# Four row buffers instead of two for the partial sums, and two buffers instead of three for the late weight words

## The chip, the cores and the metric

The kernel runs on one core of a Trainium2 chip. The metric is the device time of one execution in microseconds (us). TensorE (PE) multiplies, VectorE (DVE) and ScalarE (ACT) do elementwise work and read the accumulators out, SyncE (SP) and GpSimd (POOL) only issue transfers here.

## The reference

All inputs are float32, and wide weights are handed over as float64 words and made into float32 by the kernel. For each of 8 batches and 8 heads (576 rows, head size 64, 32 memory slots):

```python
a = softmax(phi, axis=2)                 # over the 576 rows, for each memory slot
k_m = einsum('bhsm,bhsd->bhmd', a, k)    # 32 memory keys per head
v_m = einsum('bhsm,bhsd->bhmd', a, v)
attn = softmax(q @ k_m^T / 8)
x = (attn @ v_m)  rearranged to (8*576, 512)
out = (sigmoid(x @ w_gate) * (x @ w_val)) @ w_out    # 512 -> 1536 -> 512
```

The kernel never forms `x`. It multiplies `v_m` with the weights of the gate and value layers (`make_u`), so that the gate is a product of that with the attention weights.

## The kernel before

**Tiles.** The hidden width 1536 is cut into 12 tiles of 128, `f` = 0 to 11. The 576 rows of a batch `b` are cut into four full tiles of 128 rows, `t` = 0 to 3, and a tail of 64. A step is one pair `(b, f)`. Its two halves are `c` = 0 (row tiles 0 and 1) and `c` = 1 (row tiles 2 and 3 with the tail). A half does `gate_half` (12 matmuls, a sigmoid on ACT, a product on DVE, and the split of the result into a high and a low part), and `out_half` three halves later (`LAG`): six matmuls that add into the accumulators `acc[b, t]` of two row tiles in PSUM.

**Turns.** Batches 0 to 3 do not run through all 12 tiles of the hidden width at once, since the weights are still being loaded and converted. They go in turns of `TURN` = 4 steps: batches 0 to 3 with f = 0 to 3, then again with f = 4 to 7, then with f = 8 to 11. Batches 4 to 7 then run all 12 steps each. There are 96 steps in all.

**Partial sums.** At the end of a turn the four accumulators are read out into a tile `row` (128 x 512, 256 KB) and freed for the next turn. After f = 3 the row is a plain copy (L495 on ACT, L497 on DVE) and is stored to a DRAM tile `part`. After f = 7 and f = 11 the earlier `part` is loaded into a row tile, the accumulator is added to it in place (L492 on DVE), and it is stored to `part` again or, after f = 11, to the output. The helper `row_of` allots a row tile and issues that load. In before there are two row buffers. The tiles of t = 0 and 1 are allotted and loaded at the end of the next to last step of the turn:

```python
if (b, f + 1) in ends and c:
    for t in range(2):
        rows[b, t] = row_of(b, t)
```

Those of t = 2 and 3 are allotted only when `out_half` reads the accumulator out, by `rows.pop((b, t), None) or row_of(b, t)`.

**Queues.** `move` keeps two queues, each in program order: "batch" on SP (inputs, `row<-part`, and the attention weights `at_hi`, `at_lo` that are fetched back for the next turn) and "stream" on POOL (weight words, `part<-row`, `out_dram<-row`). A transfer that waits holds up those behind it on its queue.

**Weight words.** `CONVERT` says in which step each piece `(f, k)` of the weights is converted: one ACT instruction (L171) and four on DVE (L172 to L179). `load_jobs` loads the next pieces (512 KB each) when a buffer is free; a conversion's end frees one. Early pieces use four buffers. The late ones, from (8, 2) on, use `WORDS[1]` buffers. In before these are one tile of its own named `words` and two halves of the room of `q`, which nothing else uses in that stretch. The ten late pieces are (8, 2), (9, 0), (9, 1), ... (11, 2). POOL issues the first of them earlier than the program is written, because nothing makes them wait.

**Order.** PE's order is written out by hand. On DVE and ACT a scheduler places each instruction within bounds, and so a change of buffers can move instructions there.

Of the kernel before, what the change touches and what calls it, by code (L numbers as in the profile page):

```python
# [9 lines left out]
F32 = mybir.dt.float32  # L10
F32R = mybir.dt.float32r
I32 = mybir.dt.int32
# [5 lines left out]
P = 128  # L18
B, H, S, D, M = 8, 8, 576, 64, 32
DM, DFF = 512, 1536  # L20
# [3 lines left out]
SF = 4  # L24
# [11 lines left out]
QUAD = 4  # L36
TURN = 4
ALONE = 4
WORDS = (4, 3)


CONVERT = {
# [10 lines left out]
def attn_moe_kernel(  # L53
# [15 lines left out]
    mb = ctx.enter_context(tc.tile_pool(name="moe", bufs=1))  # L69
# [14 lines left out]
    def att(shape, name, bufs=1):  # L84
        return sb.tile(shape, F32, name=name, bufs=bufs)
# [11 lines left out]
    def wo_of(f):  # L97
        return [t[:, f % NE, :] for t in wos[f // NE]]
# [14 lines left out]
    def move(dst, src, queue="batch"):  # L113


        with ExitStack() as behind:
            if queue in last_move:
                behind.enter_context(tc.issue_after(last_move[queue].ins))
            last_move[queue] = queues[queue].dma_start(dst, src)  # L119
# [15 lines left out]
    def matmul(*args, **kw):  # L135
        in_turn(nc.tensor.matmul, *args, **kw)
# [6 lines left out]
    spare_room = []  # L143
# [4 lines left out]
    def load_jobs(n=None, queue="stream"):  # L148

        while jobs and (n is None or n > 0):  # L150
            f, k = jobs[0]
            room = WORDS[len(wos) - 1]
            if (k == 2 and f // NE >= len(wos)) or len(waiting) == room:
                break
            src = wo[f] if k == 2 else wgv[f][:, 2 * k : 2 * k + 2, :].rearrange("p k n -> p (k n)")
            if len(wos) == 1:
                words = pools["conv"].tile([P, 512, 2], I32, name="words", bufs=room)
            else:
                words = spare_room[0]
                spare_room.append(spare_room.pop(0))  # L160
            move(words.rearrange("p n t -> p (n t)"), src.bitcast(I32), queue)
            words_of[f, k] = words
            waiting.append(jobs.pop(0))
            n = n and n - 1

    def to_f32(dst, f, k):


        words = words_of.pop((f, k))
        low, high, bits = words[:, :, 0], words[:, :, 1], dst.bitcast(I32)  # L170
        nc.scalar.activation(dst, high.bitcast(F32), AF.Abs)  # L171
        nc.vector.tensor_scalar(dst, dst, TINY, HUGE, op0=ALU.max, op1=ALU.min)  # L172
        nc.vector.tensor_scalar(
            bits, bits, 3, 0x3FFFFFFF, op0=ALU.logical_shift_left, op1=ALU.bitwise_and
        )
        nc.vector.scalar_tensor_tensor(  # L176
            bits, high, -0x40000000, bits, op0=ALU.bitwise_and, op1=ALU.bitwise_or
        )
        last_conv[0] = nc.vector.scalar_tensor_tensor(  # L179
            bits, low, 29, bits, op0=ALU.logical_shift_right, op1=ALU.bitwise_or  # L180
        )
        waiting.remove((f, k))
        if jobs and not waiting and jobs[0][1] == 2 and jobs[0][0] // NE >= len(wos):

            early.close()
            late = ctx.enter_context(tc.tile_pool(name="late", bufs=1))
            wos[1] = [late.tile([P, NFT - NE, DM], F32R, name=f"wo2_{part}") for part in ("hi", "lo")]
            last = ctx.enter_context(tc.tile_pool(name="conv1", bufs=1))
            q_room = att([P, NKT * S], "q").bitcast(I32)
            spare_room.append(last.tile([P, 512, 2], I32, name="words"))  # L190
            spare_room.extend(
                q_room[:, i * 1024 : (i + 1) * 1024].rearrange("p (n t) -> p n t", t=2)
                for i in range(2)
            )
        load_jobs()

    def convert(f, k):
        if k == 2:
            hi, lo = wo_of(f)
            raw = mb.tile([P, DM], F32, name="wo_raw")  # L200
            to_f32(raw, f, k)
            nc.scalar.copy(hi, raw)
            rest(lo, raw, hi)
        else:
            to_f32(wg[:, f, 2 * k : 2 * k + 2, :].rearrange("p k n -> p (k n)"), f, k)
# [270 lines left out]
    def out_half(b, f, c, at_start, at_end):  # L476

        hi, lo = G.pop((b, f, c))
        w_hi, w_lo = wo_of(f)
        for j in range(2):  # L480
            t = 2 * c + j
            if at_start:
                acc[b, t] = po.tile([P, DM], F32, name=f"acc{t}")
            ts = slice(j * P, (j + 1) * P)
            o = acc[b, t]
            matmul(o, hi[:, ts], w_hi, start=at_start, stop=False)
            matmul(o, hi[:, ts], w_lo, start=False, stop=False)
            matmul(o, lo[:, ts], w_hi, start=False, stop=at_end)
            if at_end:
                st = last_rows(t) if b == B - 1 else rows.pop((b, t), None) or row_of(b, t)  # L490
                if (b, t) in part:
                    nc.vector.tensor_tensor(st, o, st, op=ALU.add)  # L492
                    part.pop((b, t))
                elif t % 2:
                    nc.scalar.copy(st, o)  # L495
                else:
                    nc.vector.tensor_copy(st, o)  # L497
                if f == NFT - 1:
                    queue = "batch" if b == B - 1 else "stream"
                    move(out[b * S + t * P : b * S + (t + 1) * P, :], st, queue)  # L500
                else:
                    part[b, t] = dram.tile([P, DM], F32, name=f"part{b}_{t}_{f}")
                    move(part[b, t], st, "stream")
                del acc[b, t]
        if (b, f + 1) in ends and c:
            for t in range(2):
                rows[b, t] = row_of(b, t)

    rows = {}
# [2 lines left out]
    def last_rows(t):  # L512

        if not room_of_last:
            room_of_last.append(att([P, SF, 512], "kvm0"))
        return room_of_last[0][:, t, :]

    def row_of(b, t):

        st = mb.tile([P, DM], F32, name="row", bufs=2)  # L520
        if (b, t) in part:
            move(st, part[b, t])
        return st
# [215 lines left out]
    for i, (b, f, at_start, at_end) in enumerate(steps):  # L739
# [20 lines left out]
        while len(pend) >= LAG:  # L760
            out_half(*pend.pop(0))
# [4 lines left out]
        while len(pend) >= LAG:  # L766
            out_half(*pend.pop(0))
# [6 lines left out]
    for half in pend:  # L774
        out_half(*half)
# [54 lines left out]
```

## Time and profile before

| what | us |
|---|---|
| runs | 788.04, 784.37, 788.99; median 788.04 |
| the profiled execution's own time | 787.27 |
| its span, from the first to the last instruction | 785.5 |
| PE busy | 737.1 (94%) |
| DVE busy | 437.5 (56%) |
| ACT busy | 334.1 (43%) |

PE is near full occupation from about 80 us on. The first 80 us are start-up. The rows below are read as "start, duration, engine, line, operation, output<-inputs, count", with the idle time ahead of the instruction and what ended it in square brackets.

### The profile page before, as it was taken

How to read it: one execution, taken by the hardware profiler on the slowest of the kernel's cores; microseconds unless marked ns; L12 is line 12 of the kernel's file. 1: busy time of each engine (PE TensorE's matmuls, PEld its weight loads, DVE VectorE, ACT ScalarE, POOL GpSimd, SP SyncE). 2: the span in 40 equal slices, each digit the busy share in tenths (PEclk: the TensorE clock that was granted, in tenths of full speed). 3: DMA queues.
4: the chain of work that ended last, by engine and by line, in shares of the span. 5: the costliest groups of instructions: out<-in, count | busy, mean ns of one | idle time of the engine just before them, and what ended most of it. 6: DMA issues, size and time to landing. Idle time of an engine off the chain costs nothing.

```text
span 785.5 us, 13710 instructions
## 1 busy us (share of the span) xinstructions
PE 737.1 (94%) x5584; PEld 608.2 (77%) x5584; DVE 437.5 (56%) x840; ACT 334.1 (43%) x789; POOL 54.3 (7%) x104
## 2 busy tenths in 40 slices
PE   6464989999999899999999999999999999999997
PEld 4343878887788688887888888878888888888886
DVE  4778576976587575455754743365234643433422
ACT  3445463746444243332633533346333433333322
POOL 0010011111111110010110000010000000010000
PEclk9786999999999999999999999999999999999999
DMA  9664826465755353344254142002000100010002
GB/s 350 277 237 156 313 112 258 129 233 179 259 173 195 129 194 128 118 151 142 68 171 166 64 133 93 1 28 88 2 1 1 54 15 1 1 55 1 1 1 68
DMA packets 27200, 93.17 MB, mean 119 GB/s; under 512 B 3520, under 2 KB 4544, under 8 KB 25088
## 3 DMA queue, kind: packets, MB, share of 16 engines
q1 hardware_dynamic: 17440, 58.99, 20.6%
q0 software_dynamic: 9696, 33.30, 12.3%
q8 instruction: 44, 0.72, 0.4%
q14 instruction: 20, 0.16, 0.1%
HBM read 69.73 MB, written 22.54 MB: 117 GB/s over the span
## 4 chain that ended last, share of the span: by engine, by line
PE 73%; DMA 4%; DVE 2%; issue 2%; ACT 1%; POOL 0%; DVEq 0%; ACTq 0%; POOLq 0%; SPq 0%
PE pu_t L133 43%; PE acc L133 29%; DMA part<-row 2%; DMA ph<-in_phiT_dram 1%; DMA row<-part 1%; ACT L108 0%; DVE wg L176 0%; ACT sg L108 0%; DVE g_lo L123 0%; DVE sg L466 0%; DVE u_lo L123 0%; DVE zs L358 0%; DVE nmx L240 0%; DVE e L361 0%; DVE wg L179 0%
## 5 line engine op out<-in xcount | busy, mean ns | idle before, releaser
L133 PE MATMUL pu_t<-at_hi,u_hi 128*128 128x256 f32 (+1 forms) x760 | 228.3, 300 | 2.4 <-DVE sg L466 1.9
L133 PE MATMUL pu_t<-at_hi,u_lo 128*128 128x256 f32 (+1 forms) x760 | 225.0, 296 | 1.0 <-DVE u_lo L123 0.9
L133 PE MATMUL pu_t<-at_lo,u_hi 128*128 128x256 f32 (+1 forms) x760 | 225.2, 296 | 0.0
L466 DVE TENSOR_TENSOR sg<-pu_t,sg 128x256 f32<-128x256 f32 (+1 forms) x190 | 86.6, 456 | 193.8 <-ACT sg L108 114.6
L108 ACT ACTIVATE sg<-pu_t 128x256 f32<-128x256 f32 (+1 forms) x190 | 77.7, 411 | 226.3 <-PE pu_t L133 226.0
L133 PE MATMUL acc<-wo_hi,g_hi 128*128 128x512 f32 x384 | 157.1, 409 | 3.4 <-DVE row L492 3.4
L133 PEld LDWEIGHTS pu_t<-at_hi,u_hi 128*128 128x128 f32 x760 | 143.2, 188 | 13.9 <-DVE sg L466 2.2
L133 PE MATMUL acc<-wo_hi,g_lo 128*128 128x512 f32 x384 | 153.3, 399 | 0.0
L133 PE MATMUL acc<-wo_lo,g_hi 128*128 128x512 f32 x384 | 152.4, 397 | 0.0
L133 PEld LDWEIGHTS pu_t<-at_lo,u_hi 128*128 128x128 f32 x760 | 143.3, 189 | 7.2
L133 PEld LDWEIGHTS pu_t<-at_hi,u_lo 128*128 128x128 f32 x760 | 143.6, 189 | 1.6 <-DVE u_lo L123 1.6
L467 ACT CAST g_hi<-sg 128x256 fp32r<-128x256 f32 x192 | 78.1, 407 | 132.2 <-DVE sg L466 132.0
L133 PEld LDWEIGHTS acc<-wo_hi,g_hi 128*128 128x128 f32 x384 | 72.6, 189 | 52.0 <-issue 39.3
L123 DVE TENSOR_TENSOR g_lo<-sg,g_hi 128x256 fp32r<-128x256 f32 x192 | 81.0, 422 | 53.7 <-ACT g_hi L467 53.4
L133 PEld LDWEIGHTS acc<-wo_hi,g_lo 128*128 128x128 f32 x384 | 72.7, 189 | 16.7
L133 PEld LDWEIGHTS acc<-wo_lo,g_hi 128*128 128x128 f32 x384 | 72.8, 190 | 9.2
L133 PE MATMUL pu_t<-wg,vT 64*32 64x512 f32 (+1 forms) x800 | 58.2, 591 | 17.3 <-DVE wg L179 16.2
L123 DVE TENSOR_TENSOR u_lo<-pu_t,u_hi 128x512 fp32r<-128x512 f32 (+1 forms) x100 | 63.2, 664 | 4.8 <-ACT u_hi L414 3.2
L414 ACT CAST u_hi<-pu_t 128x512 fp32r<-128x512 f32 (+1 forms) x100 | 51.8, 571 | 5.5 <-PE pu_t L133 5.4
L119 POOL DMA_DIRECT2D out_dram<-row x28 | 15.2, 544 | 332.9 <-DVE row L497 227.8
L133 PEld LDWEIGHTS pu_t<-wg,vT 64*32 64x32 f32 x800 | 10.1, 106 | 28.6 <-DVE wg L179 12.8
L492 DVE TENSOR_TENSOR row<-acc,row 128x512 f32<-128x512 f32 x32 | 21.9, 688 | 13.8 <-DMA row<-part 12.9
(98 smaller groups left out, 615.8 us busy)
## 6 DMA issues: line engine op xcount, KB each, us to landing
kvm<-in_kvm_dram SPq DMA_DIRECT2D x16, 1024.0 KB, 8.0
q<-in_qT_dram SPq DMA_DIRECT2D x16, 512.0 KB, 6.3
part<-row POOLq DMA_DIRECT2D x32, 256.0 KB, 2.5
row<-part SPq DMA_DIRECT2D x32, 256.0 KB, 4.3
words<-in_wgv_dram POOLq DMA_DIRECT2D x14, 512.0 KB, 4.8
out_dram<-row POOLq DMA_DIRECT2D x28, 256.0 KB, 2.3
words<-in_wo_dram POOLq DMA_DIRECT2D x12, 512.0 KB, 5.7
ph<-in_phiT_dram SPq DMA_DIRECT2D x8, 576.0 KB, 5.6
```

The costliest lines, as they stand in the source:

```text
L108: last_act[0] = nc.scalar.activation(*args, **kw)
L119: last_move[queue] = queues[queue].dma_start(dst, src)
L123: return nc.vector.tensor_tensor(lo, x, hi.bitcast(F32), op=ALU.subtract)
L133: last_pe[0] = do(*args, **kw)
L414: nc.scalar.copy(hi[:, r, :nf], pb[r])
L466: last_prod[0] = nc.vector.tensor_tensor(prod[:, :n], ps[1][:, :n], sg[:, :n], op=ALU.mult)
L467: nc.scalar.copy(ghi, prod[:, : 2 * P])
L492: nc.vector.tensor_tensor(st, o, st, op=ALU.add)
```

## The change

The row tile gets four buffers, and all four partial sums of a turn are loaded at the end of its next to last step. The space for the two further buffers (4 KB in each partition) is that of the tile `words` of the late stage, which is dropped: late words have the two halves of the room of `q` alone.

```diff
-WORDS = (4, 3)
+WORDS = (4, 2)
...
-            last = ctx.enter_context(tc.tile_pool(name="conv1", bufs=1))
             q_room = att([P, NKT * S], "q").bitcast(I32)
-            spare_room.append(last.tile([P, 512, 2], I32, name="words"))
             spare_room.extend(
...
         if (b, f + 1) in ends and c:
-            for t in range(2):
+            for t in range(SF):
                 rows[b, t] = row_of(b, t)
...
-        st = mb.tile([P, DM], F32, name="row", bufs=2)
+        st = mb.tile([P, DM], F32, name="row", bufs=4)
```

PE has the same instructions in the same order in both kernels. On the POOL queue, from the first late piece on (`in_wo_dram` is a piece k = 2, `in_wgv_dram` a piece k = 0 or 1; `part_t_f` is the partial sum of row tile t stored after step f), before has:

```order
L119 DMA part_3_3_2146<-row 128x512
L119 DMA words<-in_wo_dram 128x1024
L119 DMA q<-in_wgv_dram 128x1024 x2
L119 DMA part_0_7_2467<-row 128x512
L119 DMA part_1_7_2473<-row 128x512
L119 DMA words<-in_wo_dram 128x1024
L119 DMA part_2_7_2526<-row 128x512
```

and the changed kernel has:

```order
L119 DMA part_3_3_2146<-row 128x512
L119 DMA q<-in_wo_dram 128x1024
L119 DMA q<-in_wgv_dram 128x1024
L119 DMA part_0_7_2466<-row 128x512
L119 DMA part_1_7_2472<-row 128x512
L119 DMA q<-in_wgv_dram 128x1024
L119 DMA part_2_7_2523<-row 128x512
```

Two late pieces, not three, are asked for at once; piece (9, 1) moves behind the first two stores of the next turn, to where piece (9, 2) stood, and so each later one moves back by one.

On DVE, at the end of the turn of batch 1 with f = 4 to 7 (`acc_2592` and `acc_2596` in before, `acc_2587` and `acc_2591` in the changed kernel, are the accumulators of t = 2 and 3), before has:

```order
L176 SCALAR_TENSOR_TENSOR wg<-q,wg 128x512
L123 TENSOR_TENSOR u_lo<-pu_t,u_hi 128x512
L179 SCALAR_TENSOR_TENSOR wg<-q,wg 128x512
L123 TENSOR_TENSOR u_lo<-pu_t,u_hi 128x512
L492 TENSOR_TENSOR row<-acc_2592,row 128x512
L466 TENSOR_TENSOR sg<-pu_t,sg 128x320
L492 TENSOR_TENSOR row<-acc_2596,row 128x512
```

and the changed kernel has:

```order
L176 SCALAR_TENSOR_TENSOR wg<-q,wg 128x512
L123 TENSOR_TENSOR u_lo<-pu_t,u_hi 128x512
L490 TENSOR_TENSOR row<-acc_2587,row 128x512
L179 SCALAR_TENSOR_TENSOR wg<-q,wg 128x512
L123 TENSOR_TENSOR u_lo<-pu_t,u_hi 128x512
L490 TENSOR_TENSOR row<-acc_2591,row 128x512
L464 TENSOR_TENSOR sg<-pu_t,sg 128x320
```

(The changed file is two lines shorter there, so that L492 of before is L490.) The addition of t = 2 moves ahead of the second half of `u_lo`, and that of t = 3 ahead of the gate product `sg`.

On ACT, in the first turn (batch 0, f = 0 to 3), the copy of t = 3 and the work for the next batch's attention weights move. Before has:

```order
L414 CAST u_hi<-pu_t 128x512 x2
L467 CAST g_hi<-sg 128x256
L495 COPY row<-acc_725 128x512
L108 ACTIVATE sg<-pu_t 128x320
L467 CAST g_hi<-sg 128x256
L472 COPY left<-sg 128x64
L108 ACTIVATE sg<-pu_t 128x256
L385 CAST at_hi<-q 128x1152
L269 COPY e<-pu_t 128x512 x2
```

and the changed kernel has:

```order
L412 CAST u_hi<-pu_t 128x512 x2
L493 COPY row<-acc_725 128x512
L465 CAST g_hi<-sg 128x256
L108 ACTIVATE sg<-pu_t 128x320
L465 CAST g_hi<-sg 128x256
L470 COPY left<-sg 128x64
L383 CAST at_hi<-q 128x1152
L267 COPY e<-pu_t 128x512 x2
L108 ACTIVATE sg<-pu_t 128x256
```

The copy of the row goes ahead of the cast `g_hi`, and one sigmoid goes behind the cast `at_hi` and the two copies `e`.

## The prediction

> **What bounds the kernel now.** I read the page's head first, then its slices.
>
> ```profile
> span 785.5 us, 13710 instructions
> PE 737.1 (94%) x5584; PEld 608.2 (77%) x5584; DVE 437.5 (56%) x840; ACT 334.1 (43%) x789; POOL 54.3 (7%) x104
> PE   6464989999999899999999999999999999999997
> ```
>
> PE sets the time. It is idle for 785.5 - 737.1 = 48.4 us. Each slice is 19.6 us; the first four read 6, 4, 6, 4, which is about 39 us of idle start-up that the change does not touch. So about 9 us of idle PE are left behind the start-up, and the one slice with an 8 (255 to 275 us) is where most of them must lie. That is the ceiling for a change that only takes waits away, plus whatever a wait costs beyond itself. Next the waits, all engines, those that touch a row and one more that I need below:
>
> ```profile
> DVE nmx L240 <- DMA ph<-in_phiT_dram: 14.0, 7, 4.0
> DVE row L492 <- DMA row<-part: 12.9, 7, 5.2
> ACT row L495 <- DMA part<-row: 4.8, 2, 4.2
> PE acc L133 <- DVE row L492: 3.4, 1, 3.4
> ```
>
> The columns are the total, the count and the longest. DVE waits seven times for a row load, 12.9 us in all, but only one wait reaches PE as a wait for a row: 3.4 us. The other six are hidden, as PE works three halves ahead of what it needs. So the 12.9 us must not be credited; only what PE loses counts. I therefore measured PE's own rhythm, by the starts of the first matmul of each `out_half`, in a calm step and at the long wait:
>
> ```profile
> 230.55 0.39 PE L133 MATMUL acc<-wo_hi,g_hi 128*128 128x512 f32 x1
> 233.38 0.40 PE L133 MATMUL acc<-wo_hi,g_hi 128*128 128x512 f32 x1
> 236.54 0.39 PE L133 MATMUL acc<-wo_hi,g_hi 128*128 128x512 f32 x1
> 240.49 0.50 PE L133 MATMUL acc<-wo_hi,g_hi 128*128 128x512 f32 x1
> 256.96 0.39 PE L133 MATMUL acc<-wo_hi,g_hi 128*128 128x512 f32 x1
> 263.38 0.79 PE L133 MATMUL acc<-wo_hi,g_hi 128*128 128x512 f32 x1 [3.43 <-DVE row L492]
> 268.13 0.39 PE L133 MATMUL acc<-wo_hi,g_hi 128*128 128x512 f32 x1
> ```
>
> Undisturbed, the intervals are 2.83, 3.16 and (with `make_u`) 3.95 us. The same two intervals from 256.96 on are 6.42 and 4.75.
>
> **The change part by part. First, the third and fourth row of the turn of batch 1 with f = 4 to 7.** The chain of work and the queues show how the wait arises:
>
> ```profile
> 244.84 14.36 SPq L119 DMA_DIRECT2D row<-part  x4
> 252.39 5.82 DMA part<-row
> 258.26 4.25 DMA row<-part
> 262.63 0.69 DVE L492 TENSOR_TENSOR row<-acc,row 128x512 f32<-128x512 f32 x1 [5.17 <-DMA row<-part]
> 264.00:265.00 1.00, 1.00 (x4) 0.81 (x3) 1.00 (x3) 1.00 (x4) 0.55 (x2) 0.50 0.29 115
> ```
>
> SP comes to the four loads at 244.84, issues two, and stands 14.36 us: the row tiles of t = 2 and 3 are those of t = 0 and 1, which must first be stored (5.82 us), then loaded again (4.25 us). DVE waits 5.17 us for it, with the gate products behind it; PE runs dry for 3.43 us. With four buffers the loads go out together at about 245 to 246.5 and the third addition, which was ready about 257, finds its row. The gain in PE's rhythm is (6.42 - 2.83) + (4.75 - 3.16) = **5.2 us**. The second bracket, 1.6 us, is the clock: the last row is the stretch 264 to 265 us, where the third number from the right, the granted clock, is 0.50. It follows the idle PE and goes with it. Below zero this term cannot go by the row wait itself, since the loads are only earlier.
>
> [...]
>
> **Second, a copy in the turn of batch 2 with f = 0 to 3**, which needs no load but a free buffer:
>
> ```profile
> 168.05 0.39 PE L133 MATMUL acc<-wo_hi,g_hi 128*128 128x512 f32 x1
> 169.80 0.69 DVE L497 COPY row<-acc 128x512 f32<-128x512 f32 x1 [2.44 <-DMA part<-row]
> 170.41 0.58 ACT L495 COPY row<-acc 128x512 f32<-128x512 f32 x1 [4.22 <-DMA part<-row]
> 172.08 0.39 PE L133 MATMUL acc<-wo_hi,g_hi 128*128 128x512 f32 x1
> ```
>
> The interval is 4.03 instead of 2.83. Both waits are for the store of the rows before; with four buffers they go: **1.2 us**. The remaining row waits I count as nothing: PE has no wait behind them, and its own 9 us are nearly used up.
>
> **Third, the late words.** At about 200 us before asks for three late pieces, the change for two. This matters because of a load that runs beside them:
>
> ```profile
> L119 POOL DMA_DIRECT2D q<-in_wgv_dram x2: 527/532/538, 199.7 to 200.3; - x2
> DMA to landing us min/median/max: 7.3/8.1/8.8
> 201.00 0.33 SPq L119 DMA_DIRECT2D ph<-in_phiT_dram  x1
> 198.00:204.00 6.00, 6.00 (x47) 5.13 (x50) 2.09 (x6) 3.21 (x9) 2.57 (x5) 1.00 0.64 201
> 204.00:210.00 6.00, 6.00 (x104) 5.53 (x93) 2.00 (x4) 0.84 (x2) 0.00 (x0) 1.00 0.89 326
> 209.27 1.35 DVE L240 TENSOR_REDUCE nmx<-ph 128x2 f32<-128x1152 f32 x1 [3.96 <-DMA ph<-in_phiT_dram]
> 207.92 0.39 PE L133 MATMUL acc<-wo_hi,g_hi 128*128 128x512 f32 x1
> 214.07 0.50 PE L133 MATMUL acc<-wo_hi,g_hi 128*128 128x512 f32 x1
> ```
>
> The third piece, issued at 200.3, lands 8.8 us later at 209.1, just as `ph` does; DVE waits 3.96 us for `ph` and then PE's interval is 6.15 instead of 3.95, a loss of 2.2 us. (The last two numbers of the stretches are the DMA engines' busy share and GB/s.) Without that piece 0.52 MB less is in flight: at 326 GB/s that is 1.6 us, but the engines were busy only 0.64 of the first six microseconds, so I take 0.64 of it, **1.0 us**, between the ends 0 (the load of `ph` has its own pace) and 2.2 (all that PE lost).
>
> **What it may cost.** From (9, 1) on, each of the eight remaining late pieces can be asked for only when the piece two before it is converted, where it was three. Its time is then from that end to its own conversion. The tightest case is piece (10, 0): its load will stand where that of (10, 1) stands now, at 244.82, beside the `at` and `row` loads of the turn's end, and its conversion begins in the step at 253.12:
>
> ```profile
> L119 POOL DMA_DIRECT2D q<-in_wgv_dram x1: 541/541/541, 238.5 to 238.5; - x1
> DMA to landing us min/median/max: 4.0/4.0/4.0
> L119 POOL DMA_DIRECT2D q<-in_wgv_dram x1: 541/541/541, 244.8 to 244.8; - x1
> DMA to landing us min/median/max: 6.8/6.8/6.8
> 253.12 0.69 ACT L171 ACTIVATE wg<-q 128x512 f32<-128x512 f32 x1
> ```
>
> Alone such a load lands after 4.0 us, in the crowd after 6.8. It has 253.12 - 244.82 = 8.3 us. Two more row loads, 0.52 MB, now run in the same crowd; at 326 GB/s they add at most 1.6 us, and 6.8 + 1.6 = 8.4 is just late, by 0.1. Two of the eight pieces meet a turn's end. So the cost is between 0 and some tenths; I take 0. A word that is late stands at the head of ACT with the cast `g_hi`, `u_hi` and the next sigmoid queued behind it, then DVE's products, then PE. [...]
>
> On the SP queue the loads of `q` for batch 4 now stand behind two more rows, which cost it two issues; they are used only at that batch's scores, a turn later. On POOL no store stands behind a word that it did not stand behind before.
>
> **The moved instructions** I cost at nothing. At the turn's end the second `u_lo` follows one addition of 0.69 us, and PE needs it only in the next step's first half, after an `out_half` and a `gate_half`. In the first turn, the sigmoid on ACT goes behind these:
>
> ```profile
> 112.61 0.38 ACT L108 ACTIVATE sg<-pu_t 128x256 f32<-128x256 f32 x1 [0.57 <-PE pu_t L133]
> 112.89 1.15 ACT L385 CAST at_hi<-q 128x1152 fp32r<-128x1152 f32 x1
> 113.93 1.07 ACT L269 COPY e<-pu_t 128x512 f32<-128x512 f32 x2
> 117.94 0.31 PE L133 MATMUL pu_t<-at_hi,u_hi 128*128 128x320 f32 x1
> ```
>
> It moves by 1.15 + 1.07 = 2.2 us. Its bank of PSUM is the fourth to come round again, and PE needs it at 117.94, after transposes, the memory sums and a half of a gate; moved, the sigmoid ends near 115.2 and its product half a microsecond later. If that cover were gone, PE would lose the 2.2.
>
> **The sum**: 5.2 + 1.2 + 1.0 = 7.4. Against the profiled execution's own 787.27 us (1.8 of it outside the span) that is 779.9. The median of the runs, 788.04, is 0.8 above that execution, and I carry this over: **780.7 us**, 0.9% less.
>
> **The rivals.**
> 1. *The long wait is in some executions only.* The runs lie 4.6 us apart, 784.37 to 788.99, about the size of that stall, and the rhythm between is regular. For it: the wait depends on two transfers in the crowd. If the lowest run is one without the stall, the change leaves it the other 2.2, and the time is 784.4 - 2.2 = 782.2, or somewhat above. Chance 0.17.
> 2. *The words take the place of the rows.* The tight pieces at the turns' ends land a microsecond or two late, at these two places, and ACT's hold reaches PE in part: 3 to 5 us come back, 784 to 786. Against it: the 8.3 us of room against 4.0 to 6.8. Chance 0.12.
> 3. *Slower: the two buffers pace the whole stretch.* Each late piece whose load takes L us holds ACT for L - 8.3, and each of the eight pieces waits on a predecessor. To eat the 7.4 us all eight must take 9.2 us, and more for a slower kernel: at L = 10, 8 x 1.7 = 13.6 us, 787 + 6 = 793.5. The slowest late load in the trace is 8.8, with three pieces and `ph` at once. Chance 0.04.
> 4. *All waits go*, as with rows early SP is never held: 9 us of idle PE and 1.6 of clock, 10.6, and the time is 777.4. For it: SP, held 14.36 us above, is free at every turn's end. Against it: some of the 9 us are table loads and weights on ACT and DVE. Chance 0.07.
> 5. *It does not do what it says*: the four loads still wait at SP, for a store of the turn before. That store is a whole turn earlier, four steps of at least 2.83 + 3.16 us, so 0.02; the time would be about 787.
>
> **How the numbers follow.** The forecast has 0.58 and reaches from 778.5 to 783 (the third term between 0 and 2.2, the runs' offset 0.8 taken or not). The range that leaves out 2 in 10 reaches to rivals 4 and 2: 777.5 to 785.5. One per cent, about what a measurement of this kernel can tell from no change, is 780.2, in the middle of the forecast: of its 0.58 I give 0.29 to each side; with rival 4 that makes faster 0.36; slower is rival 3, 0.04; the rest, 0.60, lies within 1%.
>
> **What would show it.** Right: no DVE wait for `row<-part` above 1 us at the end of batch 1's second turn, no granted clock below 0.9 behind 80 us, both intervals there back at 2.83 and 3.16; no 2.44 and 4.22 at the copies of batch 2; SP's four row loads in about 1.5 us; the wait of `nmx` near 3 instead of 3.96. Wrong: waits of ACT L171 for words or `q` in 235 to 290 us, or PE intervals of the same length as now elsewhere, which would say that PE was held by another engine that the row wait only covered.

## The result, and the profile after

| what | us |
|---|---|
| after, six runs: 780.57, 779.36, 779.55, 780.28, 780.83, 781.0 | median 780.42 |
| before, six runs beside them | median 788.17 |
| ratio of the times, with its 95% interval | 0.9896 (0.9868 to 0.9924) |
| the profiled execution's own time after | 780.57 |
| its span | 778.8 |

The changed kernel is 1.0% faster, and the prediction of 780.7 us is 0.3 us off. The head of the page and its slices (PE's busy time in tenths, and the granted clock in tenths):

```profile
span 778.8 us, 13719 instructions
PE 736.2 (95%) x5584; PEld 607.2 (78%) x5584; DVE 437.4 (56%) x840; ACT 335.0 (43%) x789; POOL 53.8 (7%) x104
PE   6564989999999999999999999999999999999997
PEclk9587999999999999999999999999999999999999
```

The single 8 among the later slices of PE is gone. PE's busy time fell by 0.9 us, its idle time by 5.8 (785.5 - 737.1 = 48.4 before, 778.8 - 736.2 = 42.6 now). The waits show whose idle time it was. This is all that PE still waits for between 80 and 785 us (total, count, longest); neither here nor among the waits of DVE is there one for the load of a row:

```profile
PE pu_t L133 <- DVE sg L464: 1.9, 1, 1.9
PE pu_t L133 <- DVE wg L179: 0.9, 1, 0.9
PE pu_t L133 <- DVE u_lo L123: 0.3, 1, 0.3
PE pu_t L133 <- DVE e L334: 0.3, 1, 0.3
PE pu_t L133 <- ACT sg L108: 0.2, 1, 0.2
```

At the end of the turn of batch 1 with f = 4 to 7 the timeline has SP's loads, the third and the fourth addition, and PE's first matmul of each `out_half`; the last row is the stretch 263 to 267 us with the granted clock third from the right:

```profile
243.45 2.11 SPq L119 DMA_DIRECT2D row<-part  x4
254.80 0.68 DVE L490 TENSOR_TENSOR row<-acc,row 128x512 f32<-128x512 f32 x1
256.59 0.68 DVE L490 TENSOR_TENSOR row<-acc,row 128x512 f32<-128x512 f32 x1
255.56 0.39 PE L133 MATMUL acc<-wo_hi,g_hi 128*128 128x512 f32 x1
258.39 0.40 PE L133 MATMUL acc<-wo_hi,g_hi 128*128 128x512 f32 x1
261.56 0.39 PE L133 MATMUL acc<-wo_hi,g_hi 128*128 128x512 f32 x1
263.00:267.00 4.00, 4.00 (x35) 2.77 (x34) 2.00 (x6) 2.26 (x5) 0.54 (x1) 1.00 0.39 131
```

SP issues its four loads in 2.11 us, not 14.36. The two additions have no bracket behind them, so DVE waits for nothing there. PE's intervals are 2.83 and 3.17 us, where they were 6.42 and 4.75, and the clock is 1.00. The two other places of the sum, the copies of batch 2 and the step behind `ph`:

```profile
168.87 0.39 PE L133 MATMUL acc<-wo_hi,g_hi 128*128 128x512 f32 x1
171.71 0.40 PE L133 MATMUL acc<-wo_hi,g_hi 128*128 128x512 f32 x1
207.86 1.35 DVE L238 TENSOR_REDUCE nmx<-ph 128x2 f32<-128x1152 f32 x1 [2.92 <-DMA ph<-in_phiT_dram]
207.56 0.39 PE L133 MATMUL acc<-wo_hi,g_hi 128*128 128x512 f32 x1
212.66 0.50 PE L133 MATMUL acc<-wo_hi,g_hi 128*128 128x512 f32 x1
```

The interval at the copies is 2.84 (it was 4.03), the one at `ph` 5.10 (it was 6.15). I put all later intervals of the two traces side by side in this way. One more differs by over half a microsecond, in the first turn. Here are PE's two starts before, the wait that lies between them, and then the same place after with ACT's cast:

```profile
112.41 0.39 PE L133 MATMUL acc<-wo_hi,g_hi 128*128 128x512 f32 x1
118.82 0.39 PE L133 MATMUL acc<-wo_hi,g_hi 128*128 128x512 f32 x1
PE pu_t L133 <- ACT e L269: 0.5, 1, 0.5
```

```profile
113.32 0.39 PE L133 MATMUL acc<-wo_hi,g_hi 128*128 128x512 f32 x1
119.13 0.39 PE L133 MATMUL acc<-wo_hi,g_hi 128*128 128x512 f32 x1
113.23 1.16 ACT L383 CAST at_hi<-q 128x1152 fp32r<-128x1152 f32 x1 [0.73 <-DVE q L379]
```

The interval falls from 6.41 to 5.81. Before, `at_hi` began 0.48 us behind PE's first row (112.89 against 112.41), after it begins 0.09 ahead of it: the sigmoid no longer stands ahead of it on ACT. `e` is ready half a microsecond earlier, and PE's wait for it is gone from the list.

| place | interval before, us | after | difference |
|---|---|---|---|
| long row wait, first interval | 6.42 | 2.83 | -3.59 |
| the same, second interval (clock) | 4.75 | 3.17 | -1.58 |
| copies of batch 2 | 4.03 | 2.84 | -1.19 |
| behind `ph` | 6.15 | 5.10 | -1.05 |
| first turn | 6.41 | 5.81 | -0.60 |

These make -8.0. The small differences elsewhere cancel to within 0.1, and the first `out_half` behind the start-up starts 1.3 us later:

```profile
60.21 0.39 PE L133 MATMUL acc<-wo_hi,g_hi 128*128 128x512 f32 x1
61.49 0.39 PE L133 MATMUL acc<-wo_hi,g_hi 128*128 128x512 f32 x1
```

(The first row is before, the second after. Over the twelve profiles of this study the start lies between 60.21 and 62.38, whatever the kernel, so the execution profiled of before was the earliest.) -8.0 + 1.3 = -6.7, which is the difference of the spans.

### The profile page after: what moved, and what is told of

The parts are those of the page before. It is cut to its first block, busy times and chain, and to the rows that moved or that the text cites. A ratio compares the mean times of both kernels' runs of the same rounds, so it can differ in the third digit from the quotient of the medians.

```text
span 778.8 us, 13719 instructions
## 1 busy us (share of the span) xinstructions
PE 736.2 (95%) x5584; PEld 607.2 (78%) x5584; DVE 437.4 (56%) x840; ACT 335.0 (43%) x789; POOL 53.8 (7%) x104
## 4 chain that ended last, share of the span: by engine, by line
PE 85%; DMA 5%; DVE 4%; ACT 3%; issue 2%; SPq 0%; POOL 0%; ACTq 0%; DVEq 0%; POOLq 0%
PE pu_t L133 51%; PE acc L133 35%; DMA q<-in_qT_dram 2%; DMA ph<-in_phiT_dram 2%; ACT L108 1%; DMA words<-in_wgv_dram 1%; ACT ph L108 1%; DVE u_lo L123 0%; SPq L119 0%; DVE nmx L238 0%; DVE e L334 0%; DVE g_lo L123 0%; DVE sg L464 0%; DVE e L344 0%; DVE e L359 0%
```

## Experiments

The theory was that of the prediction: the time comes from the row waits, the long one above all, a small part from the third late word that ran beside `ph`, and fewer word buffers cost nothing. Against it stood that the place of the loads in the program, not the buffers, does it; that the long wait is in some executions only; and that two word buffers cost something that the rows' gain hides. Each ratio is against runs of the kernel before on the same chip, whose medians were 786.53 (e1 to e4), 788.7 (e5 to e8) and 787.87 (e9, e10). The lines of the kernels keep the numbers of after or of before, depending on the file they came from.

### e1: only two word buffers

Before, without the tile `words`:

```diff
-WORDS = (4, 3)
+WORDS = (4, 2)
...
-            last = ctx.enter_context(tc.tile_pool(name="conv1", bufs=1))
...
-            spare_room.append(last.tile([P, 512, 2], I32, name="words"))
```

> Only the late words go to two buffers; the rows keep two buffers and two early loads, and DVE and ACT keep the order of before. Theory (each part of the change has its own term): PE's interval at about 208 us falls from 6.15 to about 5.1, the wait of nmx for ph from 3.96 to about 3, and both row waits stay (5.17 at the third addition of batch 1, PE's intervals 6.42 and 4.75; 4.03 at the copies of batch 2). Time 1.0 us less than before, 786 to 787.5. Rival (the crowd of transfers, not the buffers, made the row wait): the long wait shrinks here too, and 3 us or more are gained. Rival (late words cost): waits of ACT for words or q appear between 235 and 290 us and the time is above before.

Measured: 785.53 us (12 runs, 780.12 to 787.4), ratio 0.9976 (0.9954 to 0.9997). Timeline at the turn's end on DVE and PE, the clock in 262 to 263 us, then PE behind `ph`:

```profile
260.87 0.69 DVE L490 TENSOR_TENSOR row<-acc,row 128x512 f32<-128x512 f32 x1 [4.74 <-DMA row<-part]
261.62 0.79 PE L133 MATMUL acc<-wo_hi,g_hi 128*128 128x512 f32 x1 [3.02 <-DVE row L490]
262.00:263.00 1.00, 1.00 (x3) 0.78 (x3) 1.00 (x3) 1.00 (x4) 0.55 (x2) 0.50 0.05 20
208.34 0.39 PE L133 MATMUL acc<-wo_hi,g_hi 128*128 128x512 f32 x1
212.72 0.49 PE L133 MATMUL acc<-wo_hi,g_hi 128*128 128x512 f32 x1
```

The long wait is all there: one word buffer less does not shorten it. What the words bring is the interval behind `ph`: 4.38 instead of 6.15, 1.8 us where I had expected about 1, which fits the 0.24% of the runs. ACT waits for no late word. So the third word had cost PE a little, and the rest of the gain must come with the row buffers and with the instructions that move with them (the first turn keeps its 6.43 here).

### e2: four row buffers, loads left where they were

After, but with the early loads of two tiles only:

```diff
-            for t in range(SF):
+            for t in range(2):
```

> As the changed kernel (four row buffers, two word buffers), but the loads of t = 2 and 3 are asked for where before had them, at the read-out. DVE, ACT, PE and POOL have the same order as in the changed kernel; only on SP some row loads stand behind q or at loads. Theory (the free buffer is what counts, since SP then issues the load as soon as it comes to it): same time as the changed kernel, 780 to 781, no DVE wait for a row above 1 us outside the turns of batches 0 and 1 with f = 8 to 11. Rival (the early place of the loads is what counts): DVE waits 2 to 4 us for the third row in most turns and 2 to 4 us of the gain are lost, 783 to 785.

Measured: 779.88 us (4 runs, 778.91 to 780.81), ratio 0.9911 (0.9889 to 0.9933). The waits of DVE for rows in the whole execution:

```profile
DVE row L490 <- DMA row<-part: 1.5, 4, 0.7
```

This is as good as after. SP works ahead of the program: it comes to the loads of t = 2 and 3 as soon as those before them are issued (from 242.65 us, all four in 2.17 us), and a free buffer was all that it needed here. The second part of the change, the loop over all four tiles, does nothing that can be measured here.

### e3: three row buffers

e2 with one buffer less:

```diff
-        st = mb.tile([P, DM], F32, name="row", bufs=4)
+        st = mb.tile([P, DM], F32, name="row", bufs=3)
```

> As the run before it, with three row buffers. t = 2 has its own buffer, t = 3 still waits for the store of t = 0; the order on DVE, ACT, PE and POOL is that of the changed kernel. Theory (the chain store, load, addition is the cost, whichever row it holds): in the turn of batch 1 with f = 4 to 7 the third addition finds its row and the fourth waits about 4 to 5 us on DVE; PE loses again 3 to 5 us there with a clock below 1, and 1 us or less at the copies of batch 2: 783.5 to 786. Rival (the third row alone was the trouble, the fourth has time to spare): time as the changed kernel, 780 to 781.

Measured: 779.9 us (4 runs, 778.8 to 781.95), ratio 0.9916 (0.9888 to 0.9943). SP, DVE and PE at the turn's end:

```profile
242.95 12.42 SPq L119 DMA_DIRECT2D row<-part  x4
257.70 0.69 DVE L490 TENSOR_TENSOR row<-acc,row 128x512 f32<-128x512 f32 x1 [1.46 <-DMA row<-part]
255.06 0.39 PE L133 MATMUL acc<-wo_hi,g_hi 128*128 128x512 f32 x1
257.90 0.40 PE L133 MATMUL acc<-wo_hi,g_hi 128*128 128x512 f32 x1
261.07 0.39 PE L133 MATMUL acc<-wo_hi,g_hi 128*128 128x512 f32 x1
```

My expectation failed and the other one held. SP stands 12.42 us for the fourth load, almost as long as before, and DVE waits 1.46 us, yet PE's intervals are 2.84 and 3.17. With two buffers the third row has to go through a store and a load; with three only the fourth has, and that one is used later. The length of SP's hold is not what costs time; what counts is which row stands behind it, and when PE needs that row. (This execution loses 1.6 us at another place, to the clock in the first turn; the last section comes back to it.)

### e4: `nmx` held back

After, with the maximum over `ph` for one batch queued behind other DVE work, so that `ph` may land later:

```diff
-            a_max(then)
+            with behind() if b == QUAD else ExitStack():
+                a_max(then)
```

> The changed kernel with one instruction held back: the maximum over phi of batch 5 (nmx) stands on DVE behind the work of its own step, some 150 us later, not at 207 us. Theory (the load of ph holds DVE there, and with it the gate products): the interval of PE at 207.6 falls from 5.10 to about 3.95, no DVE wait for ph there, time 1.1 us below the changed kernel, about 779.3. Rival (something else, the weights or the tables, is late there): the interval stays, 780.4; or the 1.1 us come back where nmx now stands.

Measured: 778.68 us (5 runs, 777.91 to 779.3), ratio 0.9895 (0.9876 to 0.9914). The interval of PE is 4.38 us (207.01 to 211.39), not the 3.95 that the prediction had called undisturbed. e1, e2, e3 and e5 have 4.38 as well, without this edit. So 4.38 is the floor of this step, and after's 5.10 holds 0.7 us of the wait for `ph`. Other executions with two word buffers do not have them: DVE waits 1.63 us for `ph` in e1 and 1.50 in e2, against 2.92 in after. The ratios of e4 and e2 overlap, and that of after too: no gain is shown.

### e5: a late word less

After, with

```diff
-WORDS = (4, 2)
+WORDS = (4, 1)
```

> The changed kernel with one late word in flight instead of two: a late piece is asked for only when the one before it is converted. That conversion ends about 4.4 us after it began, so of a step of 6.6 us 2.2 are left for a load that lands after 3.6 to 7.3 us. Theory (a late word stands at the head of ACT, with the gate's casts behind it, and PE follows): each of the nine pieces from (9, 0) on is late by 1.4 to 5 us, ACT shows waits for q from 210 to 300 us, PE's intervals there stretch, and 13 to 45 us are lost: 793 to 825. Rival (PE's lead of three halves hides late words): a few us at most, 780 to 785.

Measured: 780.46 us (4 runs, 777.92 to 780.97), ratio 0.9888 (0.9859 to 0.9916). Far from the 793 and more that I expected, but the edit did not make the case that it was meant to make: it left both halves of the room of `q` in use, in turn. ACT's conversion of the piece (8, 2), and POOL's load of the next:

```profile
222.66 0.68 ACT L171 ACTIVATE wo_raw<-q 128x512 f32<-128x512 f32 x1
223.01 0.54 POOL L119 DMA_DIRECT2D q<-in_wgv_dram  x1
```

The load goes out while the conversion still runs, so it writes the other half. This says only that a load asked for at that moment is early enough: no wait of ACT for a word appears. The case itself is e9.

### e6: four row buffers and three word buffers

After, with the third late word in the room of `e`, which is free in that stretch:

```diff
-WORDS = (4, 2)
+WORDS = (4, 3)
...
+            e_room = att([P, 2 * S], "e").bitcast(I32)
+            spare_room.append(e_room[:, :1024].rearrange("p (n t) -> p n t", t=2))
```

> The changed kernel with a third late word buffer again, in the room of e, which is free from about 210 to 345 us; so its first load, (9, 1), goes out behind the sums of batch 4 and not at 200 us beside ph. DVE, ACT, PE and SP keep the order of the changed kernel. Theory (two buffers are enough, no late word is waited for): time as the changed kernel, 779 to 781, no wait of ACT for words in either. Rival (two buffers cost some tenths at the turns' ends that the rhythm hides): 0.5 to 1 us less.

Measured: 779.94 us (6 runs, 778.02 to 782.22), ratio 0.9887 (0.9861 to 0.9914). A third word buffer on top of four rows is worth nothing that can be measured. This is not the rows alone: the third load goes out at 211.30 us, behind `ph`, and not at 200 beside it. Four row buffers with three pieces loaded at 200 us were not run; that the words' share is the 1.8 us of e1 there too is argued.

### e7: three row buffers and `nmx` held back

e3 with the edit of e4, the version that might have beaten both.

> Three row buffers (loads of t = 2 and 3 asked for at the read-out) and nmx of batch 5 held back: both experiments together. Theory: each does here what it did alone, the time is that of the run with nmx held, 778 to 779.5, with a DVE wait of 1 to 2 us for the fourth row that PE does not see. Rival (the nmx wait had given the fourth row its time): PE waits for a row again, 780 or more.

Measured: 780.05 us (4 runs, 779.22 to 780.56), ratio 0.9888 (0.9861 to 0.9914). It is no better than after, and half a microsecond above the 778 to 779.5 that I had expected. The rival is not what the trace shows: DVE waits 1.43 us for the fourth row, and PE's intervals there are 2.84 and 3.16.

### e8: the kernel before, once more

> The kernel of before once more, one profile. Theory (the long wait is a chain of two transfers in a crowd, its price depends on whether the idle PE also loses its clock, and for how long): the DVE wait for the third row of batch 1 is again 4 to 5.5 us, PE idle near 3 us; the interval behind it lies between 3.2 (full clock) and 6. Rival (the wait is in some executions only): PE's interval is 2.83 there and the time is about 783.

One execution, 787.65 us. The first of DVE's two late additions, the PE rows that the two release, and the clock behind:

```profile
261.81 0.69 DVE L492 TENSOR_TENSOR row<-acc,row 128x512 f32<-128x512 f32 x1 [3.45 <-DMA row<-part]
262.56 0.49 PE L133 MATMUL acc<-wo_hi,g_hi 128*128 128x512 f32 x1 [1.74 <-DVE row L492]
264.50 0.49 PE L133 MATMUL acc<-wo_hi,g_hi 128*128 128x512 f32 x1 [0.97 <-DVE row L492]
266.00:267.00 1.00, 1.00 (x6) 1.00 (x5) 0.97 (x3) 0.00 (x0) 0.00 (x0) 0.50 0.54 209
```

The wait is there again, in another shape: 3.45 us on DVE, less than the 4 to 5.5 that I had expected, and two smaller ones on PE, and the clock still falls to half. The two intervals are 4.74 and 5.98, a loss of 4.7 us against 2.83 and 3.16.

### e9: one late word buffer

e5, with the second half of the room taken away:

```diff
-                for i in range(2)
+                for i in range(1)
```

> The changed kernel with one half of the room of q for all late words, so that a load really waits for the conversion ahead of it (in the run that only allowed one piece in waiting, the two halves still let the next load go). The scheduler puts the conversions later on ACT and DVE to meet this. Theory (the words pace the stretch when they are late): from one load to the next stand a conversion of about 4.4 us, 0.5 of issue and a landing of 3.6 to 7.3 us, 8.5 to 12 us against a step of 6.6, for nine pieces; ACT waits for q several times, PE's intervals stretch from 230 to 320 us, and 10 to 45 us are lost: 790 to 825. Rival (ACT and DVE have room, the weights are needed only from the third round of turns on, and lateness is hidden until then): 780 to 784, with PE held only near the first step that needs them, at about 320 us.

Measured: 788.65 us (10 runs, 787.42 to 790.69), ratio 1.0009 (0.9994 to 1.0024). ACT's waits for late words, and PE at the place where it loses most:

```profile
ACT wg L171 <- DMA q<-in_wgv_dram: 17.4, 6, 3.9
ACT wo_raw L171 <- DMA q<-in_wo_dram: 12.4, 3, 5.9
295.19 0.50 PE L133 MATMUL acc<-wo_hi,g_hi 128*128 128x512 f32 x1
300.06 0.63 PE L133 MATMUL pu_t<-at_hi,u_hi 128*128 128x320 f32 x1 [2.33 <-DVE sg L464]
301.83 0.63 PE L133 MATMUL acc<-wo_hi,g_hi 128*128 128x512 f32 x1
```

One buffer gives the whole gain back, some 8 us, and by the mechanism of the prediction's third rival: ACT stands for late words nine times, 29.8 us in all, and PE's rhythm loses behind it (6.64 us here, 3.4 more than after: 2.33 us of idle PE, and most of the rest is slower matmuls: from 300.50 to 301.83 us those of 320 columns start 0.27 us apart, where 0.15 is usual in this trace). Over the whole stretch PE loses about 10 us, a third of what ACT waits. My number for it, 790 at least, was too high, since all of ACT's waiting was put on PE; the rival's 780 to 784 was too low.

### e10: before, with `nmx` held back

The edit of e4 in the kernel before, with three words and two rows.

> The kernel of before (two row buffers, three late word buffers) with nmx of batch 5 held back on DVE. Theory (the third late word costs PE only by making ph late under nmx): the interval of PE at 208 us falls from 6.15 to 4.4 with the three words still loaded at once, 1 to 1.8 us less than before; both row waits stay. Rival (the words delay something else there): the interval stays near 6 and so does the time.

Measured: 784.46 us (12 runs, 780.79 to 788.11), ratio 0.9956 (0.9934 to 0.9977). PE behind `ph`, then DVE and PE at the long wait, and the clock:

```profile
207.49 0.39 PE L133 MATMUL acc<-wo_hi,g_hi 128*128 128x512 f32 x1
211.87 0.49 PE L133 MATMUL acc<-wo_hi,g_hi 128*128 128x512 f32 x1
260.28 0.69 DVE L492 TENSOR_TENSOR row<-acc,row 128x512 f32<-128x512 f32 x1 [5.00 <-DMA row<-part]
261.02 0.50 PE L133 MATMUL acc<-wo_hi,g_hi 128*128 128x512 f32 x1 [3.27 <-DVE row L492]
260.00:262.00 2.00, 0.97 (x3) 0.49 (x3) 1.72 (x4) 0.60 (x3) 0.54 (x1) 1.00 0.06 24
```

The time is 0.44% below before, 3.4 us, and 1.8 at the near end of its interval, where I had expected 1 to 1.8. The interval of PE is 4.38, as in e1, though the three words are loaded beside `ph` as before. So the loss behind `ph` is DVE standing at the head of its queue for `nmx`, and either edit takes it away: fewer words in flight, or other work put ahead. The long wait stays (3.27 us of idle PE), and here the clock did not fall.

## Why the prediction was right

**The long wait: right.** The 5.2 us came as 3.59 + 1.58 = 5.17, both from the place and by the cause that the chain showed. Which part of the change does it was not told apart: four buffers and early loads were treated as one thing, and e2 and e3 show that the place of the loads counts for nothing that can be measured and that three buffers are enough. Before's 3.43 us of idle PE went with 3.4 us at half clock; e1's shorter 3.02 us went with 6.8, and its two intervals lost 5.9 us, more than before's.

**The copies of batch 2: right.** 1.2 us were taken, 1.19 measured. The waits of 2.44 and 4.22 us for stores are gone. In e1 and e8, with two row buffers, the interval is 3.63 and 3.68, so that the match to the tenth is luck here too.

**The late words beside `ph`: right in cause, and 1.0 against a measured 1.05 by luck.** The wait of `nmx` is 2.92 where I had said near 3, but the working behind the 1.0, 1.6 us by the busy share of the DMA engines, has no support: in e1 the same edit gave 1.77, also within the bounds of 0 and 2.2. The upper bound was itself too high, as the floor is 4.38 and not 3.95.

**The cost of fewer word buffers: right at 0, with the tight spot less tight.** The load of the piece that stood at 8.3 us of room, now issued at 243.4, landed after:

```profile
DMA to landing us min/median/max: 7.0/7.0/7.0
```

7.0 us, where it was 6.8: two more row loads in SP's queue cost POOL's load 0.2 us, not up to 1.6. The same load takes 6.8 in all four profiles with two row buffers, and 6.9, 6.9 and 7.1 in e2, e4 and e6, which have four. The word at the next turn's end went from 7.0 to 7.3. The sum of bytes that I had taken as the upper end, 1.6 us, is not what these numbers show; why such a load needs 7 us in the crowd and 4.0 alone, no run here takes apart.

**The moved instructions: wrong.** I cost them at nothing and looked only for harm to the sigmoid that moves back. What moved ahead of it, `at_hi` and `e`, was what PE waited for, 0.5 us of it, and the first turn became 0.60 shorter. The cast and the copies ran in the same order in e2 to e7 and e9, with intervals of about 5.8, and in the old order in e1, e8 and e10, with 6.41 to 6.43.

**The sum** came out close in part by chance. In the traces the places give 8.0 us, not 7.4, and the span of the profiled execution fell by 6.7 only, as its start-up was 1.3 later. The medians, 788.17 and 780.42, are 7.75 apart. The largest term is the least steady one, as the rivals below show, so that it met 5.2 is luck in part too: it was worked out from one execution.

**The rivals.** The first, a wait in some executions only, is not what the profiles show: all four with two row buffers have it. Its price is not steady, though: PE loses 5.17 (before), 5.9 (e1), 4.7 (e8) and 3.8 us (e10) there. That would fit the wider spread of the runs, 4.6 us before against 1.6 after, though e6, with four row buffers, spreads over 4.2. The fastest runs with two row buffers, 780.1 in e1 and 780.8 in e10, have no profile; e1's profile is that of its slowest run. The four fastest of its twelve, 780.1 to 782.6, have mean granted clocks of 0.980 to 0.985, the other eight 0.968 to 0.978, so they lost less to the clock somewhere, the start-up included. Whether they lack the wait stays open, and with it the rival in part. The second and the third ask for late words that came in time. e9 shows that the third's mechanism is real one buffer lower, where eight microseconds of cost take 29.8 us of waits on ACT, so its rule (each late microsecond on ACT is one of the time) was about three times too dear. The fourth did not come: PE still waits 3.6 us by its list. The fifth is refuted by SP's 2.11 us, though I had said 1.5 for the four issues.

In the profile after, the clock never fell below 0.9 in a slice behind 80 us, as was said.

## What to carry to other kernels

Credit a removed wait only with what the engine that sets the time loses behind it: DVE waited 12.9 us for rows, and PE's rhythm, taken from the starts of one repeating matmul, lost 5.2 of it with the clock included. The loads on SP's queue went as early as their buffers allowed, wherever the program wrote them (e2: all four in 2.17 us, like after's 2.11); so count the buffers first, find the smallest number at which no row that is needed soon still has to go through a store and a load (here three: the fourth row does, in time), and then look one below, where the cost can begin steeply (two word buffers: nothing, one: 8 us). Where a scheduler moves instructions, ask not only what the one moved back delays, but what the ones moved ahead release.

## What the runs showed of the hardware

The granted clock did not follow the length of PE's idle time alone. In the first turn before, after, e3, e9 and e10 have the same gap of PE, 1.90 us of waiting for `sg` near 108 us. In before and after the clock stays at 1.00 behind it and PE's interval is 3.71 us, as it is in e10. In e3 the clock falls to half and the interval is 5.3; in e9 it is 5.28, with starts of matmuls 0.43 us apart instead of 0.23. In e3 the gap and the stretch 110 to 111 us are:

```profile
107.90 0.41 PE L133 MATMUL pu_t<-at_hi,u_hi 128*128 128x320 f32 x1 [1.90 <-DVE sg L464]
110.00:111.00 1.00, 1.00 (x3) 0.68 (x3) 1.00 (x3) 0.00 (x0) 0.00 (x0) 0.50 0.67 262
```

The table has the idle time of PE at these places and the granted clock read behind it. The last column is worked out from the stretches of one microsecond in which the clock changed, each taken as a mix of 1.00 and 0.50 (before: 0.61 in 263 to 264 us and 0.68 in 266 to 267; e1: 0.90 in 260 to 261 and 0.69 in 267 to 268; e8: 0.61 in 265 to 266 and 0.68 in 268 to 269).

| run and place | PE idle, us | granted clock behind it | at half for, us |
|---|---|---|---|
| before, long wait | 3.43 | 0.50 | 3.4 |
| e10, long wait | 3.27 | 1.00 | 0 |
| e1, long wait | 3.02 | 0.50 | 6.8 |
| e8, long wait | 1.74 and 0.97 | 0.50 | 3.4 |
| e3, first turn | 1.90 | 0.50 | at least 1 |
| before and after, first turn | 1.90 | 1.00 | 0 |

So like waits had unlike prices: e10's 3.27 us kept the clock, e1's 3.02 lost it for 6.8 us, and 1.90 us at one and the same place lost it in e3 but not in before and after. What decides between them is not shown by these runs.

The loads of the rows became slower, and that cost nothing. The median time from issue to landing of the 32 loads `row<-part`, of 256 KB each, is 4.3 us before and 5.7 after. With four out at once the median load takes 1.4 us longer, while the waits are gone: the second pair no longer follows the first through a store and the same two buffers.
